# New engine rules in a planner, and its order of instructions searched again, in an attention and maxout kernel on one core

## The chip, the cores and the metric

The kernel runs on one core of one Trainium2 chip. The metric is device time in microseconds (us) of one execution. A run executes the kernel several times; medians are compared.

## The reference, cut to what matters

There are 4 batches, 8 heads, 768 positions and a head width of 64. Heads 0, 2 and 6 attend to all earlier positions, the other five only to the first 4 positions and to a window of 64. What the heads give is laid side by side (3072 rows of 512) and goes through a maxout block.

```python
scores = q @ k.T / 8                      # per batch and head, masked: causal, or causal and (sink or window)
a = exp(scores - max); a /= sum(a)        # softmax
x = (a @ v) -> rows (batch, position), columns (head, width): 3072 x 512
g = maximum(x @ w1, x @ w2)               # 3072 x 1024
out = g @ w_out                           # 3072 x 512
```

The kernel uses max(h1, h2) = h2 + relu(h1 - h2), so that out = relu(x (w1 - w2)) w_out + x (w2 w_out).

## The kernel before, in words

**Work.** All of it stands in `tile_paired_heads`. Heads go in pairs: index `n` runs over 16 pairs (4 of each batch; `HP` is 4). A pair's kind says whether its heads are full (F) or streaming (S). For each pair:

- `prepare_qk` loads q and k in float32, casts them to bfloat16 (`qkf` to `qb`) and turns them so that the head width lies on the partitions (`qk`). The casts of batch 0 (`cast_first_qk`, 128x192 each) may run on GpSimd, VectorE or ScalarE; those of later batches (`cast_qk`, 128x768) run on GpSimd alone. Up to `n` = 4 TensorE turns them through PSUM and a copy takes them out (`unturn`); later pairs use a VectorE transpose (`turn_squares`). For streaming heads `mix_k` copies parts of `qk` into `kx`: two copies, on VectorE or GpSimd.
- `prepare_v` loads v and casts it into `vb` (`cast_first_v` or `cast_v`); `mix_v` makes two copies from `vb` into `vx` on GpSimd.
- `attend` queues score matmuls (`ps`, line 624; the masks of batch 0 are added as bias matmuls, line 598), the exponential on ScalarE (`at`, line 641), mask products on VectorE in the later batches (line 663), the matmuls with v (`po`, line 685), and on VectorE a reciprocal and two multiplications (lines 700 and 702), which give `x`.

At the end of each batch `x` is transposed, by TensorE (`turn_x`, line 718) or, in batch 3, by a VectorE transpose (line 728) and 16 small DMAs for each half (`regroup_x`). Then the rows go through `up` (`ph`, line 759), a relu on ScalarE or VectorE (`g`, lines 770 and 772), `down` (`pout`, line 786), a copy out of PSUM and a store. The weights are prepared on the way, while batch 0 runs: `prepare_w` loads quarters of w2 and w1, subtracts them (`subtract`, line 893, two pieces for each quarter, on VectorE or GpSimd) and casts w2 (`cast_w2`); `prepare_wo` casts w_out (`cast_wo`); `product` multiplies w2 by w_out (line 866). The functions for copies share two lines: 421 (VectorE or GpSimd) and 419 (ScalarE).

**Order.** Nothing is scheduled by the compiler; every engine executes its instructions in the order in which they were issued. That order comes from a planner in the kernel file, `Order`. Each step is an `Op` with a cost in us for each engine that may run it, its dependencies and a rank (the pair's number, mostly). `Order.plan` walks through a modelled time: an engine that is free takes the ready operation of lowest rank, on the engine on which it would end first; TensorE picks from named lists ("TX", "S", "W", "TQ", "F", "P"), and up to 33 us of the modelled time it may run unneeded matmuls from list "D" (line 900) where nothing else fits. Loads are issued by SyncE in the order of the program. The modelled times only set the order; on the chip semaphores make each instruction wait for its data.

`Order.vary` shifts ranks before the plan is made. For each number in `SEEDS` it draws 1 to 20 operations that don't belong to TensorE, and mostly adds a normally distributed shift to their ranks:

```python
        for seed in seeds:
            rng = random.Random(seed)
            for o in rng.sample(movable, rng.choice((1, 2, 4, 8, 20))):
                o.shift = o.shift + rng.gauss(0, 2.0) if rng.random() < 0.8 else 0.0
```

**VectorE and GpSimd in the planner before.** An `Op` can be marked `port`. Every GpSimd operation, marked or not, starts no earlier than 0.13 us before the end of the last `port` operation on VectorE; a `port` operation on VectorE starts no earlier than 0.13 us before the end of the last GpSimd operation. Marked are `subtract`, `cast_first_qk`, `cast_first_v`, `mix_k` and the mask products. An engine is free again when the whole cost of an operation has passed.

Of the kernel before, what the change touches and what calls it, by code (L numbers as in the profile page):

```python
# [16 lines left out]
ACT = mybir.ActivationFunctionType  # L17
# [93 lines left out]
def heads_of(slots):  # L111
# [9 lines left out]
TERMS_FROM = {("s", 1, 2): 0, ("d", 3): 128, ("d", 5): 128, ("s", 0, 0): 640}  # L121
WARM, FIRST, FIRST_LOADS = 90, 6, 3


SEEDS = (
# [6 lines left out]
)  # L132


class Op:


    def __init__(self, engine, cost, emit, deps=(), rank=0, tail=0.12, bank=False, issue=0.55, by="SP", single=False, port=False):
        self.cost = cost if isinstance(cost, dict) else {engine: cost}
        self.engine, self.emit, self.rank, self.tail = engine, emit, rank, tail  # L140
        self.deps, self.bank = [d for d in deps if d is not None], bank
        self.issue, self.by, self.single, self.port = issue, by, single, port
        self.end, self.ready, self.users = None, 0.0, []
        self.behind, self.followers = None, []


class Order:

# [57 lines left out]
    def plan(self, names, together=(), spare=(), until=0.0, slack=0.0, begin=None):  # L206
# [71 lines left out]
        while True:  # L278
            while waiting and waiting[0][0] <= t:
                pending.append(heapq.heappop(waiting)[2])  # L280
            times = [waiting[0][0]] if waiting else []
            done = False
            for e in ("ACT", "DVE", "POOL", "SP"):
                able = [o for o in pending if e in o.cost or (o.engine == "DMA" and o.by == e)]
                if not able:
                    continue
                if free[e] > t:
                    times.append(free[e])
                    continue
                for o in sorted(able, key=lambda o: (o.rank + o.shift, o.ready, o.number)):  # L290
                    if o.engine == "DMA":
                        free[e] = t + o.issue
                        start = max(free[e], free["DMA"])
                        free["DMA"] = start + o.cost["DMA"]
                        end = free["DMA"] + 0.75
                    else:
                        shared = e == "POOL" or e == "DVE" and o.port
                        begin = max(t, held["DVE" if e == "POOL" else "POOL"] - 0.13) if shared else t
                        end = begin + o.cost[e]
                        if any(max(free[x], t) + c < end for x, c in o.cost.items() if x != e):  # L300
                            continue
                        free[e] = end
                        if shared:
                            held[e] = end
                    pending.remove(o)
                    steps.append((o, e, None))
                    release(o.followers, t)
                    finish(o, end)
                    done = True
                    break  # L310
            if free["PE"] <= t:
                best = pick()
                if best and best[1] <= t:
                    n = best[0]
                    now = t
                    for k in range(2 if n in together and not self.lists[n][at[n]].single else 1):
                        mine = self.lists[n][at[n]:at[n] + 1]
                        w = when(mine[0]) if mine else None
                        if w is None or w > now + 0.3:
                            break  # L320
                        o = mine[0]
                        at[n] += 1
                        bank = None
                        if o.bank:
                            bank = free_bank()[1]
                            users[bank] = o.bank
                        steps.append((o, "PE", bank))
                        now += o.cost["PE"] * (2 if now < self.warm else 1)
                        finish(o, now)
                    free["PE"] = now  # L330
                    done = True
                elif best:
                    times.append(best[1])
            else:
                times.append(free["PE"])
            if done:
                continue
            later = [x for x in times if x > t]
            if not later:
                break  # L340
            t = min(later)
# [6 lines left out]
def tile_paired_heads(tc, q, k, v, w1, w2, wo, out, qkf, vf, tab, idle, heads):  # L348
# [561 lines left out]
    def prepare_w(c, rank):  # L910
        loaded = load(1.5, load_w2(c))
        old, frees = take("qn")
        T["w1f", c] = slot("qn")[:, 0:KC * 256].rearrange("p (c f) -> p c f", c=KC)
        o = load(1.5, load_w1(c), old)
        for two in range(2):
            subs[c, two] = op(
                None, {"DVE": 0.69, "POOL": 1.27}, subtract(c, two), [o, loaded], rank=rank, port=True,
            )
            frees.append(subs[c, two])
        cast = op(None, {"DVE": 0.7, "POOL": 1.05}, cast_w2(c), [loaded], rank=rank)  # L920
        w2_casts.append(cast)
        ev = op(None, {"DVE": 0.69, "ACT": 1.05}, take_w2(c), rank=rank)
        ev.deps = [pe("P", 0.6, turn_w2(c), [cast], bank=ev)]
        w2t_ops.append(ev)
# [4 lines left out]
    def prepare_qk(n, part=0):  # L929
        nb, rank = len(parts_of[n][part]), rank_of(n, part)  # L930
        old, bfrees = take("qb")
        if n < HP:
            for ts in ((0,), (1,)):
                cost = {"POOL": 0.35, "DVE": 0.28, "ACT": 0.36} if len(ts) == 1 else {"POOL": 0.52, "DVE": 0.36, "ACT": 0.52}
                mine = [
                    op(
                        None, cost, cast_first_qk(n, part, hh, ts),
                        [*(first[part][t] for t in ts), *old], rank=rank, port=True,
                    ) for hh in range(2)
                ]  # L940
                for t in ts:
                    casts[n, part, t] = mine
                    first_frees[part][t].extend(mine)
        else:
            qn_old, frees = take("qn")
            T["qn", n, part] = slot("qn").rearrange("p (t s) -> p t s", t=2)
            cost, issue = (0.55, 0.52) if n < TURNED else (1.32, 1.14)
            mine = {
                (t, hh): load(cost, load_qk(n, part, t, hh), [*qn_old, sorted_], issue=issue)
                for t in range(2) for hh in range(2)  # L950
            }
            for t in range(2):
                casts[n, part, t] = [
                    op("POOL", 0.84, cast_qk(n, t), [mine[t, 0], mine[t, 1], *old], rank=rank)
                ]
                frees.extend(casts[n, part, t])
# [15 lines left out]
            ready.append(un)  # L972
        if "S" in KINDS[n] and part + 1 == len(parts_of[n]):
            cost = {"DVE": 0.5, "POOL": 0.92} if nb == NB else {"DVE": 0.4, "POOL": 0.6}
            ready.append(op(None, cost, mix_k(n), [*ready], rank=rank, port=True))
        k_ready[n] = [*k_ready.get(n, ()), *ready]

    def prepare_v(n, part=0):
# [3 lines left out]
        if n < HP:  # L982
            mine = [
                op(
                    None, {"POOL": 0.35, "DVE": 0.29}, cast_first_v(n, part, hh),
                    [first[part][2], *done_with["v", n][0]], rank=rank, port=True,
                ) for hh in range(2)
            ]
            first_frees[part][2].extend(mine)
        else:  # L990
            old, frees = take("vn")
            T["vn", n, part] = slot("vn").rearrange("p (h n d) -> p h n d", h=2, d=D)
            loads = [load(0.84, load_v(n, part, hh), [*old, sorted_], issue=0.57) for hh in range(2)]
            mine = [op("POOL", 0.84, cast_v(n), [*loads, *done_with["v", n][0]], rank=rank)]
            frees.extend(mine)
        v_ready[n] = [*v_ready.get(n, ()), *mine]
        if "S" in KINDS[n] and part + 1 == len(parts_of[n]):
            cost = (0.49 if KINDS[n] == "FS" else 0.78) * (1 if nb == NB else 0.7)
            v_ready[n] += [
                op("POOL", cost, mix_v(n, lower), [*mine], rank=rank) for lower in (True, False)  # L1000
            ]

    frees_ps = []
# [34 lines left out]
    def weigh(n, half, rank):  # L1038
# [17 lines left out]
        if p == HP - 1 and b >= SQUARES_FROM:  # L1056
# [6 lines left out]
            if half == 1 or not whole:  # L1063
# [2 lines left out]
                    op(  # L1066
                        "DMA", 0.5 if whole else 0.25, regroup_x(b, rows, g, a),
                        [*turned[b], *done_with["xt", b][0]], rank=n + 4 * half, issue=0.66,
                        by=("SP", "ACT")[a % 2], tail=0.5,
                    ) for g in range(4) for a in range(4)  # L1070
                ]
                done_with["xs", b][1].extend(moved)
# [11 lines left out]
    def prepare_wo(c, rank):  # L1084
        old, frees = take("qn")
        T["wof", c] = slot("qn")[:, 0:2 * d_model].rearrange("p (e f) -> p e f", e=2)
        o = load(1.4, load_wo(c), old)
        cost = {"ACT": 1.05, "DVE": 0.7, "POOL": 1.2}
        wob_ops.append(op(None, cost, cast_wo(c), [o], rank=rank))
        frees.append(wob_ops[-1])  # L1090

    def prepare_first(part, n):
# [668 lines left out]
```

## Time and profile before

| what | value |
|---|---|
| median of 3 runs | 184.31 us (183.98 to 184.77) |
| the profiled execution | 184.63 us |
| its span, first to last instruction | 182.8 us |
| granted TensorE clock | 0.998 |
| TensorE (PE) busy | 171.7 us, 94% of the span |
| VectorE (DVE) busy | 117.9 us, 65% |
| ScalarE (ACT) busy | 108.3 us, 59% |
| GpSimd (POOL) busy | 66.4 us, 36% |

How to read it: the profile is one execution. The span is 1.83 us shorter than the time of that execution, which in turn is 0.32 us above the median. Busy time counts an instruction from start to end, so pipelined matmuls that overlap count once. "PEld" is TensorE's loading of weights, "SPq" SyncE's queue of DMA issues. Of a wait the profile names the instruction that came last.

### The profile page before, as it was taken

How to read it: one execution, taken by the hardware profiler on the slowest of the kernel's cores; microseconds unless marked ns; L12 is line 12 of the kernel's file. 1: busy time of each engine (PE TensorE's matmuls, PEld its weight loads, DVE VectorE, ACT ScalarE, POOL GpSimd, SP SyncE). 2: the span in 40 equal slices, each digit the busy share in tenths (PEclk: the TensorE clock that was granted, in tenths of full speed). 3: DMA queues.
4: the chain of work that ended last, by engine and by line, in shares of the span. 5: the costliest groups of instructions: out<-in, count | busy, mean ns of one | idle time of the engine just before them, and what ended most of it. 6: DMA issues, size and time to landing. Idle time of an engine off the chain costs nothing.

```text
span 182.8 us, 4751 instructions
## 1 busy us (share of the span) xinstructions
PE 171.7 (94%) x1683; PEld 97.0 (53%) x1683; DVE 117.9 (65%) x265; ACT 108.3 (59%) x163; POOL 66.4 (36%) x108
## 2 busy tenths in 40 slices
PE   6899897989999899999989999999999999999990
PEld 1365564556454455566445655666555545545460
DVE  2687959991397789899798989979767632000000
ACT  3197797866956267875736695899673300526410
POOL 2244687504354955345774356683000000000000
PEclk9999999999999999999999999999999999999999
DMA  5999999699899799799998998999112368312032
GB/s 173 307 266 351 230 322 387 218 308 258 139 171 198 118 196 204 127 192 170 177 191 163 152 194 159 158 346 403 37 57 113 43 64 170 74 73 103 0 117 72
DMA packets 120674, 32.90 MB, mean 180 GB/s; under 512 B 107586, under 2 KB 116546, under 8 KB 120642
## 3 DMA queue, kind: packets, MB, share of 16 engines
q1 hardware_dynamic: 113954, 31.73, 74.6%
q10 hardware_dynamic: 6688, 0.79, 2.9%
q8 instruction: 15, 0.25, 0.6%
q14 instruction: 17, 0.14, 0.3%
HBM read 25.43 MB, written 6.29 MB: 174 GB/s over the span
## 4 chain that ended last, share of the span: by engine, by line
PE 58%; SPq 17%; DMA 12%; DVE 5%; issue 4%; POOL 2%; ACT 0%; POOLq 0%
PE pout L786 23%; PE ph L759 19%; SPq L476 9%; SPq L1616 7%; PE ps L624 5%; PE po L685 4%; DMA w2f<-in_moe_w_dram 3%; DMA vf<-in_v_dram 3%; DMA qkf<-in_q_dram 3%; PE po L866 3%; DMA qkf<-in_k_dram 2%; SPq L487 2%; PE pout L801 1%; DVE kx L421 1%; PE px L718 1%
## 5 line engine op out<-in xcount | busy, mean ns | idle before, releaser
L641 ACT ACTIVATE at<-ps 128x1024 bf16<-128x1024 f32 (+2 forms) x64 | 59.9, 978 | 12.5 <-PE ps L624 12.4
L759 PE MATMUL ph<-xt,w 128*128 128x384 bf16 x256 | 45.8, 326 | 1.1 <-DVE x L702 1.0
L786 PE MATMUL pout<-wob,g 128*128 128x512 bf16 x184 | 44.8, 379 | 0.0
L770 ACT ACTIVATE g<-ph 128x384 bf16<-128x384 f32 x56 | 26.8, 491 | 22.5 <-DMA out_dram<-ot 11.1
L421 POOL CAST qb<-qkf 128x768 bf16<-128x768 f32 (+1 forms) x37 | 24.1, 661 | 32.3 <-DMA qkf<-in_k_dram 17.1
L759 PEld LDWEIGHTS <-w 128*128 128x128 bf16 x256 | 23.6, 98 | 16.8 <-DVE x L702 1.3
L663 DVE TENSOR_TENSOR at<-at,tab 128x1024 bf16<-128x1024 bf16 (+5 forms) x45 | 27.3, 633 | 4.5 <-ACT at L641 4.2
L786 PEld LDWEIGHTS <-g 128*128 128x128 bf16 x184 | 16.7, 98 | 18.2
L702 DVE TENSOR_TENSOR x<-po,rez 128x192 f32 x64 | 22.9, 358 | 2.4 <-DVE x L702 0.2
L564 DVE STREAM_TRANSPOSE qk<-qb 128x768 bf16<-128x768 bf16 x22 | 20.8, 963 | 5.0 <-POOL qb L421 5.0
L786 PE MATMUL pout<-w2o,xt 128*128 128x512 bf16 x92 | 23.7, 380 | 0.0
L685 PEld LDWEIGHTS <-at 128*128 128x128 bf16 x477 | 19.1, 98 | 7.2 <-issue 0.5
L624 PE MATMUL ps<-qk 64*128 64x128 bf16 (+2 forms) x307 | 21.7, 234 | 0.0
L685 PE MATMUL po<-vb,at 128*128 128x65 bf16 x387 | 21.7, 194 | 0.1
L421 DVE COPY ot<-pout 128x512 f32<-128x512 f32 (+1 forms) x4 | 2.5, 625 | 29.3 <-PE pout L801 23.4
L421 POOL CAST vb<-vf 128x768 bf16<-128x768 f32 (+1 forms) x21 | 13.7, 666 | 17.5 <-DMA vf<-in_v_dram 13.2
L624 PEld LDWEIGHTS <-qk 64*128 64x128 bf16 x307 | 11.6, 94 | 13.2 <-issue 10.6
L421 POOL COPY vx<-vb 64x650 bf16<-64x650 bf16 (+3 forms) x24 | 16.3, 682 | 1.2
L419 ACT COPY ot<-pout 128x512 f32<-128x512 f32 (+1 forms) x9 | 5.1, 562 | 16.0 <-PE pout L786 12.0
L786 PEld LDWEIGHTS <-xt 128*128 128x128 bf16 x92 | 8.2, 98 | 8.5 <-issue 0.2
L624 PE MATMUL ps<-qk,kx 64*128 64x128 bf16 x91 | 9.2, 216 | 2.6 <-POOL kx L421 1.7
L772 DVE TENSOR_SCALAR g<-ph 128x384 bf16<-128x384 f32 x8 | 4.4, 555 | 7.0 <-PE ph L759 6.9
(66 smaller groups left out, 152.7 us busy)
## 6 DMA issues: line engine op xcount, KB each, us to landing
vf<-in_v_dram SPq DMA_DIRECT2D x24, 192.0 KB, 3.4
qkf<-in_q_dram SPq DMA_DIRECT2D x44, 96.0 KB, 3.2
qkf<-in_k_dram SPq DMA_DIRECT2D x44, 96.0 KB, 2.4
out_dram<-ot SPq DMA_DIRECT2D x11, 256.0 KB, 2.0
w2f<-in_moe_w_dram SPq DMA_DIRECT2D x4, 512.0 KB, 7.3
qkf<-in_moe_w_dram SPq DMA_DIRECT2D x4, 512.0 KB, 9.0
qkf<-in_moe_w_out_dram SPq DMA_DIRECT2D x4, 512.0 KB, 4.5
out_dram<-w2f SPq DMA_DIRECT2D x8, 256.0 KB, 4.5
```

Source lines behind the costliest of these rows:

```text
L421: eng[e].tensor_copy(out=out, in_=in_)
L476: dma[e].dma_start(out=dst[64 * hh + a:64 * hh + a + 32].rearrange("p (j e) -> p j e", e=32), in_=src[:, :, a:a + 32].rearrange("o (j p) e ...
L564: nc.vector.transpose(T["qk", n][:, t], T["qb", n, 0][:, t])
L624: nc.tensor.matmul(ps[:, bank, e * 128:(e + wide) * 128], lhsT=lhsT, rhs=qk[rows, 0, i * 128:(i + wide) * 128], start=bank not in begun, s ...
L641: nc.scalar.activation(out=at[:, 0:len(w), 0:w[0]], in_=T["ps", n, t][:, 0:len(w), 0:w[0]], func=ACT.Exp, scale=scale,)
L663: eng[e].tensor_tensor(out=at, in0=at, in1=tbl, op=ALU.mult)
L685: nc.tensor.matmul(po[:, hh, b[-1] - 3 * half, :], lhsT=at[:, bank, e * 128:(e + 1) * 128], rhs=rhs, start=first and (bank, hh, e, b) == m ...
L702: nc.vector.tensor_tensor(out=T["x", b][:, 3 * half:3 * half + 3, bass.ds(heads[PLACES[n][hh]], 1), :], in0=po[:, hh, :, 0:D].unsqueeze(2) ...
L759: nc.tensor.matmul(ph, lhsT=w12[:, kc, fc * 128:(fc + 1) * 128], rhs=xts[b % len(xts)][:, 3 * tg:3 * tg + 3, kc, :], start=(kc == 0), stop ...
L770: nc.scalar.activation(out=g[:, fc, :], in_=ph, func=ACT.Relu)
L786: nc.tensor.matmul(pout, lhsT=lhsT, rhs=rhs, start=(e == 0), stop=(e == len(steps) - 1))
L1616: lambda engine, dst=dst, src=src: engine.dma_start(out=dst, in_=src) for dst, src in pieces
```

## The change

The planner's rules and some costs are changed, and 67 numbers are put behind the 80 of `SEEDS`. No function that emits instructions is changed; the tiles, the sizes and the work are the same. What can differ on the chip is the order on each engine, and for operations with several engines, which one runs them.

- A new mark `shy`. A GpSimd operation waits for VectorE's `port` operations in the model only if it is `shy`: `subtract`, `mix_k`, `cast_first_v`, `cast_v` and `mix_v` are. The GpSimd casts `cast_qk`, `cast_first_qk`, `cast_w2` and `cast_wo` no longer wait. VectorE's `port` operations still wait for any GpSimd operation.
- `cast_w2` and `cast_wo` become `port`; `cast_first_qk` no longer is.
- An engine is free again a little before an operation's end: 0.1 us on ScalarE, 0.08 us on VectorE, 0.05 us on GpSimd.
- Costs: `cast_first_qk` on VectorE from 0.28 to 0.345 us, `cast_first_v` on VectorE from 0.29 to 0.28 us, `cast_wo` on GpSimd from 1.2 to 1.05 us; the time after a `regroup_x` DMA from 0.5 to 1.2 us.

```diff
+OVERLAP = {"ACT": 0.1, "DVE": 0.08, "POOL": 0.05}
...
-    230371,
+    230371, 7, 12, 23, 30, 37, 50, 56, 63, 71, 77, 81, 96, 103, 131, 133, 156, 211, 221, 229, 261,
...
+    442954, 442986, 443032, 443084, 443252,
...
-                        shared = e == "POOL" or e == "DVE" and o.port
-                        begin = max(t, held["DVE" if e == "POOL" else "POOL"] - 0.13) if shared else t
+                        other = {"POOL": "DVE" if o.shy else None, "DVE": "POOL" if o.port else None}.get(e)
+                        begin = max(t, held[other] - 0.13) if other else t
                         end = begin + o.cost[e]
                         if any(max(free[x], t) + c < end for x, c in o.cost.items() if x != e):
                             continue
-                        free[e] = end
-                        if shared:
+                        free[e] = end - OVERLAP[e]
+                        if e == "POOL" or e == "DVE" and o.port:
                             held[e] = end
...
-                None, {"DVE": 0.69, "POOL": 1.27}, subtract(c, two), [o, loaded], rank=rank, port=True,
+                None, {"DVE": 0.69, "POOL": 1.27}, subtract(c, two), [o, loaded], rank=rank, port=True, shy=True,
...
-        cast = op(None, {"DVE": 0.7, "POOL": 1.05}, cast_w2(c), [loaded], rank=rank)
+        cast = op(None, {"DVE": 0.7, "POOL": 1.05}, cast_w2(c), [loaded], rank=rank, port=True)
...
-                cost = {"POOL": 0.35, "DVE": 0.28, "ACT": 0.36} if len(ts) == 1 else {"POOL": 0.52, "DVE": 0.36, "ACT": 0.52}
+                cost = {"POOL": 0.35, "DVE": 0.345, "ACT": 0.36}
...
-                        [*(first[part][t] for t in ts), *old], rank=rank, port=True,
+                        [*(first[part][t] for t in ts), *old], rank=rank,
...
-            ready.append(op(None, cost, mix_k(n), [*ready], rank=rank, port=True))
+            ready.append(op(None, cost, mix_k(n), [*ready], rank=rank, port=True, shy=True))
...
-                    None, {"POOL": 0.35, "DVE": 0.29}, cast_first_v(n, part, hh),
-                    [first[part][2], *done_with["v", n][0]], rank=rank, port=True,
+                    None, {"POOL": 0.35, "DVE": 0.28}, cast_first_v(n, part, hh),
+                    [first[part][2], *done_with["v", n][0]], rank=rank, port=True, shy=True,
...
-            mine = [op("POOL", 0.84, cast_v(n), [*loads, *done_with["v", n][0]], rank=rank)]
+            mine = [op("POOL", 0.84, cast_v(n), [*loads, *done_with["v", n][0]], rank=rank, shy=True)]
...
-                op("POOL", cost, mix_v(n, lower), [*mine], rank=rank) for lower in (True, False)
+                op("POOL", cost, mix_v(n, lower), [*mine], rank=rank, shy=True) for lower in (True, False)
...
-                        by=("SP", "ACT")[a % 2], tail=0.5,
+                        by=("SP", "ACT")[a % 2], tail=1.2,
...
-        cost = {"ACT": 1.05, "DVE": 0.7, "POOL": 1.2}
-        wob_ops.append(op(None, cost, cast_wo(c), [o], rank=rank))
+        cost = {"ACT": 1.05, "DVE": 0.7, "POOL": 1.05}
+        wob_ops.append(op(None, cost, cast_wo(c), [o], rank=rank, port=True))
```

More of the change, by code (lines that the diff above doesn't have):

```diff
@@ L130, with __init__ @@
     101142, 101161, 101196, 101554, 101575, 101777, 101808, 101856, 102175, 102430, 102706, 230301,
[1 row of a table removed]
[5 rows of a table added]
 )
 class Op:
-    def __init__(self, engine, cost, emit, deps=(), rank=0, tail=0.12, bank=False, issue=0.55, by="SP", single=False, port=False):
+    def __init__(self, engine, cost, emit, deps=(), rank=0, tail=0.12, bank=False, issue=0.55, by="SP", single=False, port=False, shy=False):
         self.cost = cost if isinstance(cost, dict) else {engine: cost}
@@ L141, in __init__ @@
         self.deps, self.bank = [d for d in deps if d is not None], bank
-        self.issue, self.by, self.single, self.port = issue, by, single, port
+        self.issue, self.by, self.single, self.port, self.shy = issue, by, single, port, shy
         self.end, self.ready, self.users = None, 0.0, []
```

3 rows, old and new, of the table SEEDS are left out of this document.

## The prediction

> **What bounds the kernel now.** I read the page first. TensorE is the bound: busy 94% of the span, with its full clock in every slice, and the chain that ended last closes with its matmuls.
>
> ```profile
> PE 171.7 (94%) x1683; PEld 97.0 (53%) x1683; DVE 117.9 (65%) x265; ACT 108.3 (59%) x163; POOL 66.4 (36%) x108
> PEclk9999999999999999999999999999999999999999
> ```
>
> The order changes neither number nor size of the needed matmuls, so only TensorE's waits can go or come. I then asked for the busy time by stretches, from its first needed matmuls (about 9 us) to its last (178.4 us); the columns after the length are PE, PEld, DVE, ACT and POOL busy.
>
> ```profile
> 9.00:20.00 11.00, 10.51 (x150) 6.42 (x150) 8.98 (x28) 8.96 (x17) 4.45 (x14) 1.00 1.15 307
> 20.00:30.00 10.00, 8.89 (x137) 5.58 (x138) 7.91 (x20) 8.64 (x11) 8.94 (x20) 1.00 1.01 299
> 30.00:40.00 10.00, 8.92 (x110) 5.92 (x109) 9.79 (x19) 7.22 (x13) 3.22 (x3) 1.00 0.82 285
> ...
> 60.00:70.00 10.00, 9.33 (x88) 4.90 (x87) 8.13 (x17) 4.95 (x6) 7.51 (x11) 1.00 0.94 160
> ...
> 90.00:100.00 10.00, 8.94 (x93) 4.74 (x92) 9.20 (x19) 5.01 (x5) 6.78 (x9) 1.00 0.99 180
> ```
>
> TensorE's idle time is 0.49 + 1.11 + 1.08 + 0.67 + 1.06 = 4.41 us; the stretches left out have none. That is all an order can win, save three unneeded matmuls between 11 and 14 us, about 0.2 us each. The timeline of TensorE shows the four large waits:
>
> ```profile
> 28.89 0.23 PE L624 MATMUL ps<-qk,kx 64*128 64x128 bf16 x2 [0.89 <-DVE kx L421]
> 37.18 0.82 PE L759 MATMUL ph<-xt,w 128*128 128x384 bf16 x4 [0.95 <-DVE x L702]
> 64.06 0.23 PE L624 MATMUL ps<-qk,kx 64*128 64x128 bf16 x1 [0.67 <-POOL kx L421]
> 92.07 0.23 PE L624 MATMUL ps<-qk,kx 64*128 64x128 bf16 x1 [1.06 <-POOL kx L421]
> ```
>
> Last I read what VectorE and GpSimd did ahead of them.
>
> ```profile
> 26.93 1.18 DVE L421 CAST w2b<-w2f 128x1024 bf16<-128x1024 f32 x1 [1.28 <-DMA w2f<-in_moe_w_dram]
> 32.86 3.37 DVE L893 TENSOR_TENSOR w<-qkf,w2f 128x512 bf16<-128x512 f32 x3
> 89.36 2.34 DVE L663 TENSOR_TENSOR at<-at,tab 128x768 bf16<-128x768 bf16 x2
> 89.61 0.82 POOL L421 CAST qb<-qkf 128x768 bf16<-128x768 f32 x1
> 90.50 1.52 POOL L421 COPY kx<-qk 64x320 bf16<-64x320 bf16 x2
> ```
>
> Two kinds of delay can be seen: a queue whose head waits for a load (the 1.28 us before w2b), and VectorE and GpSimd standing in each other's way. The w2b cast took 1.18 us; the cast of w_out of the same size took 0.69 us on VectorE. The three subtractions took 3.37 us; alone one takes 0.67. The kx copies took 1.52 us; the same two took 0.85 us at 63 us. The cast at 89.61 kept its 0.82 us while the masks beside it were late: the first took 1.48 us, where the shortest of its size takes 0.52.
>
> **The change part by part.** The sum goes against the profiled execution: 184.63 us, of which 182.8 are the span. It was 0.32 us above the median of 184.31, and the median gets the difference.
>
> *Does the new rule fit the rows better?* Of the 24 GpSimd casts of 128x768 to qb, 23 took 0.82 to 0.83 us whatever VectorE did; one took 1.00, at 70.8 us beside a mask. VectorE's casts of 128x192 to qb took 0.342 to 0.354 us with GpSimd's equal casts running beside them (at 6.0, 8.5 and 17.0 us): the old plan forbade that and priced them at 0.28; the new one allows it at 0.345. Masks and copies on VectorE do wait for GpSimd: over their shortest durations, kx copies (0.23) took 1.33 and 1.31 us more twice, a mask of 128x512 (0.38) 1.33 more. The early release fits too: two VectorE casts start 0.26 us apart at 0.34 each, and a pair of 0.35 us on GpSimd starts 0.29 apart. So the planner's clock for these two engines now stands nearer the chip's.
>
> The Trainium skill, in "SBUF — State Buffer", section "Who interferes with whom", says that VectorE and GpSimd share one port pair, that the first to take it holds it for the whole instruction, and that the other fully blocks. By that a GpSimd cast would wait for a mask that began first, against the new rule; the row at 70.8 us agrees, where 0.17 us was added.
>
> *Terms.*
> 1. The wait at 28 us: the planner of before let w2b run on VectorE without regard to GpSimd; it now waits, so its real price is seen. Worth 1.18 - 0.69 = 0.49 of the 0.89; the rest is the late load, which no edit prices anew.
> 2. The wait at 92 us: the casts in front of kx no longer queue behind masks in the plan, and the masks do behind casts. Worth 1.52 - 0.85 = 0.67 of the 1.06.
> 3. The wait at 37 us: the subtractions were marked for contention already. One stood for 1.76 us beside a GpSimd subtraction of 1.27 that had itself waited 0.40 us for its load. Bounds 0 and 0.95; I take 0, since that rule is as before.
> 4. The wait at 64 us: kx ran at its undisturbed 0.85 us, behind a cast whose data had just landed. I take 0 of 0.67.
> 5. 9 to 20 us: waits of 0.49 and fillers of 0.6. Landings of q, k and v set most of the pace (VectorE and GpSimd both start at 12.15 to 12.18 us, when v lands). Bounds 0 and 1.1; I take 0.3, nearer to no gain.
> 6. New waits: every later order is redrawn by 67 new seeds and by the free times, and loads land as before. Bounds: none, or two of the largest seen, 2.1 us. I take one of the small kind, 0.2, as the early waits on casts were (0.20, 0.22, 0.23).
> 7. The regroup's 1.2 us tail, and the costs of w_out's and first v's casts: 0. The 16 first regroup DMAs (0.59 to 0.75 us of issue each but for two, on two queues, after a transpose that begins at 140.07) land by about 149.8 us; TensorE is busy until 152.3 with rows of batch 2, so 2.5 us of cover. If that cover is gone, each us beyond it costs one.
>
> Sum: -0.49 - 0.67 - 0.30 + 0.20 = -1.26. The profiled execution would come to 183.37 us, the median to 184.31 - 1.26, about 183.05. Item 7 is also a ceiling: unless attention ends earlier, TensorE gains at most 2.5 us before it waits for the regroup, which gives 181.8.
>
> **The rivals.**
> - *The waits only move* (a seed removes one kx wait and puts another operation before the next). For it: the waits at 28 and 64 us begin with a load, whose costs are unchanged, and a shift that helps one copy delays another. Against it: after 40 us TensorE waits in two places only, 1.7 us in 138, so there is other work to put in front. Terms 1, 2 and 5 give 1.46 and new waits of 1.3 take it back: 184.15.
> - *The casts do wait.* The port rule holds whenever a mask begins first, and the plan, believing otherwise, packs casts beside masks. The largest such loss in the rows is a cast of v at 59.4 us, 1.22 instead of 0.83 us: 0.39. Two such ahead of the two kx chains cost 0.8: -1.26 + 0.8, so 183.9. Against it: only 5 of 36 large casts lost anything, 0.05 to 0.39 us each.
> - *Slower: a weight piece stands at the head of VectorE's queue before it has landed.* From 19 to 41 us VectorE or GpSimd must do 8 subtractions, 4 casts of w2 and some of w_out, and behind them wait kx, the reciprocals and x. The new plan frees VectorE 0.08 us earlier for each of some 60 operations by then, yet its loads are priced as before, so it reaches these pieces with the loads where they were. It happened once: 1.28 us of waiting became 0.89 on TensorE, whose remaining work there is short. From about 0.4 us (1.28 - 0.89) of lateness on it reaches TensorE. Two more such waits at 0.89 to 0.95 each, with nothing won: 184.31 + 1.84, 186.15. For it: DMA share is 1.0 there and w2 took 7.3 us to land. Against it: the pieces may also go to GpSimd, idle 6.8 of the 10 us from 30 to 40.
>
> **How the numbers follow.** About 0.5% (0.9 us) is what a measurement of this kernel can tell from no change. Forecast, faster: 0.53; its own range is 181.8 (ceiling) to 183.4. Waits only move: 0.11; casts do wait: 0.07; both lie within 0.5%, together 0.18. Slower by weight pieces: 0.29. It has a good chance since nothing in the new rules prices landings, and two of the four large waits start there. The range runs from the ceiling to near the slower rival: 181.7 to 186.0.
>
> **What would show it.** If right: no wait over 0.5 us on kx near 28 and 92 us; the two-copy kx groups nearer to 0.85 us; fewer VectorE rows stretched beyond 1.3 us; more GpSimd casts beside VectorE casts before 20 us; TensorE idle 9 to 178 us near 3.2 us. If slower: a new bracketed DMA wait of VectorE between 19 and 41 us, and a TensorE wait behind it. It would be wrong in kind if TensorE waited at the first rows of batch 3 for the regroup, or if its unneeded matmuls (18 now) grew past 20 us.

## The result, and the profile after

The kernel after takes 185.66 us (median of 22 runs, 184.28 to 187.78), the kernel before 184.53 us in the runs beside it. The ratio is 1.0065 with a 95% interval of 1.0036 to 1.0094: slower, by less than 1% but clear of no change. The ratios and their intervals are taken from executions within 1.5% of the fastest of the same kernel, the medians from all. The profiled execution took 184.81 us, its span is 183.0 us.

Of the after kernel's page, the same two lines as before, which show almost no change (23 of TensorE's matmul records are missing in this trace, 1660 instead of 1683, so its busy time is a little low, here and in the stretches that follow):

```profile
PE 171.0 (93%) x1660; PEld 97.4 (53%) x1682; DVE 115.2 (63%) x273; ACT 108.2 (59%) x165; POOL 63.1 (34%) x98
PEclk9999999999999999999999999999999999999997
```

Of the after kernel's windows, the same stretches (columns: PE, PEld, DVE, ACT, POOL busy, then granted clock, DMA share, GB/s):

```profile
9.00:20.00 11.00, 9.66 (x144) 6.05 (x145) 8.34 (x29) 9.08 (x18) 3.29 (x11) 1.00 1.15 307
20.00:30.00 10.00, 8.26 (x111) 5.18 (x111) 9.23 (x22) 8.09 (x12) 6.11 (x12) 1.00 0.98 283
30.00:40.00 10.00, 9.62 (x143) 6.93 (x141) 9.65 (x22) 7.29 (x11) 6.27 (x6) 1.00 0.86 311
...
60.00:70.00 10.00, 9.89 (x89) 4.90 (x89) 6.28 (x18) 5.52 (x8) 6.02 (x10) 1.00 0.90 154
70.00:90.00 20.00, 18.99 (x239) 11.62 (x237) 18.06 (x38) 14.71 (x21) 9.46 (x12) 1.00 0.96 169
90.00:100.00 10.00, 8.99 (x85) 4.73 (x84) 9.76 (x24) 5.30 (x7) 5.48 (x9) 1.00 0.96 172
```

TensorE gains 0.70 us from 30 to 40 us and 0.56 from 60 to 70. It loses 0.85 from 9 to 20, 0.63 from 20 to 30 and 1.01 from 70 to 90 us, where it had been busy throughout; the waits that its timeline names there are 0.75 us of the 1.01, the rest may be missing records. The timeline shows the large waits of after. The four shown of before are gone or below 0.25 us, but near 92 us another stands in place of the one for kx:

```profile
16.37 0.34 PE L557 MATMUL pt<-tab,qb 128*128 128x128 bf16 x3 [0.72 <-POOL qb L428]
23.74 0.33 PE L557 MATMUL pt<-tab,qb 128*128 128x128 bf16 x3 [1.59 <-DVE qk L428]
88.92 0.81 PE L766 MATMUL ph<-xt,w 128*128 128x384 bf16 x4 [0.43 <-DVE g L779]
92.00 0.20 PE L692 MATMUL po<-vb,at 128*128 128x65 bf16 x1 [0.79 <-DVE at L670]
```

VectorE's rows ahead of that last wait:

```profile
89.78 0.56 DVE L428 COPY kx<-qk 64x320 bf16<-64x320 bf16 x2
90.37 1.57 DVE L670 TENSOR_TENSOR at<-at,tab 128x1024 bf16<-128x1024 bf16 x1
```

The longest, before 23.74, is a turn that needs a PSUM bank, which VectorE's copy to `qk` frees. What VectorE, and then GpSimd, did ahead of it (timeline of the kernel after):

```profile
21.43 1.79 DVE L900 TENSOR_TENSOR w<-qkf,w2f 128x512 bf16<-128x512 f32 x1 [0.64 <-DMA qkf<-in_moe_w_dram]
23.14 0.54 DVE L428 COPY qk<-pt 128x384 bf16<-128x384 bf16 x1
23.61 0.67 DVE L428 COPY xt<-px 128x1024 bf16<-128x1024 bf16 x1
```

```profile
21.41 1.27 POOL L900 TENSOR_TENSOR w<-qkf,w2f 128x512 bf16<-128x512 f32 x1 [0.30 <-DMA qkf<-in_moe_w_dram]
```

VectorE has its first subtraction at the head of its queue before the w1 piece has landed and waits 0.64 us for it. The same landing releases GpSimd's subtraction of the other half; GpSimd starts 0.02 us earlier, runs its usual 1.27 us, and VectorE's takes 1.79 instead of about 0.7. The copies that TensorE waits for stand behind it. In the kernel before, VectorE did them first:

```profile
21.00 1.02 DVE L421 COPY qk<-pt 128x384 bf16<-128x384 bf16 x2
22.02 1.08 DVE L421 COPY xt<-px 128x1024 bf16<-128x1024 bf16 x2
23.01 0.73 DVE L893 TENSOR_TENSOR w<-qkf,w2f 128x512 bf16<-128x512 f32 x1
```

That profile shows no drop of the clock near 25 us, and its time is 0.18 us above the profiled execution of before. It is one of 3 among 22 runs whose mean granted clock was 0.992 or more; the other 19 lay below. The experiments show what that is.

### The profile page after: what moved, and what is told of

The parts are those of the page before. It is cut to its first block, busy times and chain, and to the rows that moved or that the text cites. A ratio compares the mean times of both kernels' runs of the same rounds, so it can differ in the third digit from the quotient of the medians.

```text
span 183.0 us, 4723 instructions
## 1 busy us (share of the span) xinstructions
PE 171.0 (93%) x1660; PEld 97.4 (53%) x1682; DVE 115.2 (63%) x273; ACT 108.2 (59%) x165; POOL 63.1 (34%) x98
## 4 chain that ended last, share of the span: by engine, by line
PE 51%; SPq 17%; DMA 15%; DVE 7%; issue 5%; POOL 2%; ACT 0%; POOLq 0%; DVEq 0%
PE pout L793 23%; PE ph L766 16%; SPq L483 11%; DMA vf<-in_v_dram 6%; DMA qkf<-in_moe_w_dram 5%; PE po L692 4%; PE ps L631 4%; SPq L494 3%; SPq L1623 3%; DVE at L670 2%; DMA qkf<-in_k_dram 2%; DMA qkf<-in_q_dram 2%; DVE w L900 2%; PE pout L808 1%; POOL qb L428 1%
## 5 line engine op out<-in xcount | busy, mean ns | idle before, releaser
L793 PE MATMUL pout<-wob,g 128*128 128x512 bf16 x176 | 43.2, 379 | 0.5
L777 ACT ACTIVATE g<-ph 128x384 bf16<-128x384 f32 x50 | 24.5, 492 | 7.6 <-PE ph L766 7.4
L670 DVE TENSOR_TENSOR at<-at,tab 128x1024 bf16<-128x1024 bf16 (+5 forms) x45 | 26.2, 601 | 2.8 <-ACT at L648 2.7
L426 ACT COPY ot<-pout 128x512 f32<-128x512 f32 (+1 forms) x11 | 6.2, 567 | 30.5 <-PE pout L793 15.9
L793 PE MATMUL pout<-w2o,xt 128*128 128x512 bf16 x84 | 22.7, 379 | 0.5 <-issue 0.2
L692 PEld LDWEIGHTS <-at 128*128 128x128 bf16 x477 | 18.3, 97 | 8.0 <-DVE at L670 2.2
L428 DVE COPY ot<-pout 128x512 f32<-128x512 f32 (+1 forms) x2 | 1.1, 558 | 31.2 <-PE pout L808 29.1
L428 POOL CAST vb<-vf 128x768 bf16<-128x768 f32 (+1 forms) x16 | 11.6, 730 | 17.8 <-DMA vf<-in_v_dram 9.2
L779 DVE TENSOR_SCALAR g<-ph 128x384 bf16<-128x384 f32 x14 | 7.7, 551 | 6.0 <-PE ph L766 5.1
L426 ACT COPY w2f<-pout 128x512 f32<-128x512 f32 x7 | 4.1, 586 | 9.5 <-PE pout L793 9.5
```

The costliest lines, as they stand in the source:

```text
L426: nc.scalar.copy(out=out, in_=in_)
L428: eng[e].tensor_copy(out=out, in_=in_)
L670: eng[e].tensor_tensor(out=at, in0=at, in1=tbl, op=ALU.mult)
L692: nc.tensor.matmul(po[:, hh, b[-1] - 3 * half, :], lhsT=at[:, bank, e * 128:(e + 1) * 128], rhs=rhs, start=first and (bank, hh, e, b) == m ...
L777: nc.scalar.activation(out=g[:, fc, :], in_=ph, func=ACT.Relu)
L793: nc.tensor.matmul(pout, lhsT=lhsT, rhs=rhs, start=(e == 0), stop=(e == len(steps) - 1))
```

## The experiments

Theory A at the start: the loss is the wait near 22 us, made by the subtraction's place. Rivals: the seeds' new order elsewhere, and GpSimd's casts. The traces leave little to the casts: 31 of the 36 GpSimd casts of 128x768 take 0.82 to 0.83 us in `after` as in before, and all 36 together 31.0 us instead of 30.6. Each ratio is against the kernel before, run on the same chip.

**Rules or seeds.** `rules_only` is the kernel after with the 80 numbers of before in `SEEDS`; `seeds_only` is the kernel before with all 147.

> The changed kernel with the 80 seeds of before: the new rules and costs alone. If the rules themselves make the order worse: ratio 1.004 or more. If the new rank shifts do: ratio within 0.004 of 1. The order is a third one, so the place of its waits decides; theory A expects a wait of over 0.8 us only where VectorE or GpSimd reaches a weight piece or a first cast ahead of its landing.

> The kernel before with all 147 seeds under the old rules. The added shifts were not chosen for these rules, so they act as random ones: I expect waits like those of any order, 5 to 7 us of TensorE's idle time after 9 us, ratio 1.002 to 1.012. If the added seeds alone carry the loss, its ratio is at least that of the change, 1.0065.

Measured: 187.06 us, 1.0144 (1.0091 to 1.0196), and 186.46 us, 1.0146 (1.0102 to 1.0191). `rules_only` has the same meeting at 21.43 and 21.45 us, and TensorE waits 1.94 us behind it:

```profile
21.45 1.79 DVE L896 TENSOR_TENSOR w<-qkf,w2f 128x512 bf16<-128x512 f32 x1 [0.85 <-DMA qkf<-in_moe_w_dram]
```

So the rules and costs put the subtraction there, not the seeds. `seeds_only` has no such place and no TensorE wait over 0.96 us; its last matmul ends at 180.3 us against 178.4 before. Its trace shows where most of that can lie: it runs 24 unneeded matmuls instead of 18, some of them among needed ones at 23 to 24 us:

```profile
23.13 0.78 PE L904 MATMUL unused<-idle,tab 128*128 128x512 bf16 x2
24.17 0.39 PE L904 MATMUL unused<-idle,tab 128*128 128x512 bf16 x1
```

From 9 us on they take 3.00 us of TensorE, against 1.15 before. Such time counts as busy and is no wait. A run of this order without them was not made, so this stays argued. Each half alone measures worse than both together.

**The subtraction's place.** `later` moves it in after behind the copies, in the list of steps that `Order.run` emits; `early` moves it in before ahead of two qk copies and the x copy.

```diff
+        steps.insert(141, steps.pop(124))      # later
+        steps.insert(123, steps.pop(144))      # early
```

> The changed kernel with one VectorE subtraction (first weight quarter, first piece) moved in VectorE's order from ahead of the qk and x copies at 21.4 us to behind them and the kx copy; nothing else moves. Theory A (VectorE waits 0.64 us for the landing of w1 and then 1.1 us behind GpSimd's subtraction, and TensorE's 1.59 us wait at 22 us comes from it): that wait falls under 0.4 us and the time comes back by 1.2 to 1.6 us, to a ratio of 0.998 to 1.002 against the kernel before. Theory B (the loss lies in many small waits or in a lower granted clock): under 0.4 us, ratio 1.004 to 1.008.

> The kernel before with the same subtraction moved the other way, ahead of the two qk copies and the x copy, to the place that it has in the changed order. Theory A: a TensorE wait of 0.8 to 1.6 us appears between 21 and 24 us, ratio 1.004 to 1.009. Theory B: no wait over 0.4 us there, ratio within 0.002 of 1.

Measured: `later` 184.37 us, 0.9998 (0.9963 to 1.0034), so this one move takes the whole loss back. VectorE's subtraction, now behind the copies, waits for nothing and is short:

```profile
22.88 0.72 DVE L901 TENSOR_TENSOR w<-qkf,w2f 128x512 bf16<-128x512 f32 x1
```

The wait at 22 us is gone, but the gain is not there either: two other waits come up. One is 1.38 us before 33.41, where GpSimd's copies to vx stand behind a cast of w2 that waited 4.40 us for its load. The other is 0.94 us before 38.73, behind a later subtraction of VectorE that takes 1.74 us because GpSimd's, at 35.66, began 0.07 us ahead of it. `early` 184.51 us, 0.9997 (0.9961 to 1.0034): no loss. There VectorE started first, at 21.20, and GpSimd's subtraction was the one that took 1.77 us:

```profile
21.20 0.69 DVE L894 TENSOR_TENSOR w<-qkf,w2f 128x512 bf16<-128x512 f32 x1 [0.19 <-DMA qkf<-in_moe_w_dram]
...
21.25 1.77 POOL L894 TENSOR_TENSOR w<-qkf,w2f 128x512 bf16<-128x512 f32 x1 [0.54 <-DMA qkf<-in_moe_w_dram]
```

The early place alone is thus no loss here, though VectorE waited only 0.19 us for the landing, less than in after. Whether it becomes one when GpSimd goes first is the next question.

**Who goes first.** `win` leaves after's order but gives GpSimd an unneeded 0.52 us memset ahead of its subtraction, so that VectorE starts first. `both` adds a second memset ahead of the GpSimd cast of `qk` data at 90.6 us, so that VectorE's mask there starts before it; `both_again` is `both` once more; `again` is the kernel after.

```diff
+        late = steps[133][0]                    # win; both: also steps[524][0]
         for o, e, self.bank in steps:
+            if o is late:
+                self.hold()                     # nc.gpsimd.memset(spare, 0.0), 128x512 bf16
             o.emit(e)
```

> The changed kernel with one unneeded memset (128x512, about 0.5 us) on GpSimd ahead of its first subtraction, so that VectorE's subtraction, released by the same landing, starts first. If the loss at 22 us is mostly the shared port: VectorE's subtraction takes 0.7 instead of 1.8 us, TensorE's wait there falls from 1.59 to 0.4 to 0.7, ratio 0.999 to 1.004. If it is mostly the late landing: the wait stays over 1.2 us and the ratio at 1.004 to 1.009.

> As the run with one spare memset, with a second one on GpSimd ahead of the cast that follows the vx copies at 90.6 us, so that VectorE's mask gets the port between them. Theory A for that place: the mask of 1.57 us takes under 1.1, TensorE's wait of 0.79 us at 91 us falls under 0.3, ratio 0.003 to 0.005 under the run with one memset. Rival: the wait there comes from late loads of k, and stays.

> The changed kernel itself once more, for a second profile and a ratio on the same chip as the three beside it. All theories: ratio 1.004 to 1.009. Theory A (weight pieces at the heads of queues, with VectorE and GpSimd falling on one landing): a TensorE wait between 21 and 24 us of either about 0.4 us, where VectorE's subtraction takes 0.7, or about 1.6, where it takes 1.8.

> The changed kernel with the two spare memsets, once more. It had 0.9975 with an interval on both sides of 1. Theory A: ratio 0.993 to 0.999, both subtractions' order and the mask at 90 us as in its first profile. Rival: it is no better than the kernel before, 0.999 to 1.003.

Measured on one chip: `again` 185.44 us, 1.008 (1.0041 to 1.0118); `win` 184.67, 0.9991 (0.9946 to 1.0037); `both` 184.42, 0.9975 (0.9926 to 1.0024). `both_again`, later: 185.17, 1.0029 (0.9987 to 1.0071). In `win` VectorE's subtraction takes 0.69 us and GpSimd's 1.73:

```profile
21.41 0.69 DVE L903 TENSOR_TENSOR w<-qkf,w2f 128x512 bf16<-128x512 f32 x1 [1.30 <-DMA qkf<-in_moe_w_dram]
22.02 0.55 DVE L431 COPY qk<-pt 128x384 bf16<-128x384 bf16 x1
```

The landing's share of the wait stays (VectorE waited 1.30 us for it; TensorE 1.15, between the two values that were expected, and 2.39 in `again`), and the meeting goes VectorE's way. With it most or all of the loss goes: the medians of `win` and `both`, which share the first memset, are 0.77 and 1.02 us below `again`. The kernel before had a median of 183.94 us beside them, so a rest of up to half a per cent is not excluded. The second memset did what it should to the mask (0.79 instead of 1.57 us), but the two measurements of `both` lie on both sides of 1: its worth is not resolved, and `both_again` fell short of the 0.993 to 0.999 that was expected.

**The same meeting in the kernel before.** `blocked` moves VectorE's subtraction in before to step 131 instead of 123; `lose` is `early` with an unneeded VectorE memset ahead of the subtraction. Both were meant to let GpSimd's subtraction go first.

> The kernel before with its first VectorE subtraction moved ahead of one qk copy and the x copies, but behind another qk copy, so that GpSimd's subtraction has started when VectorE arrives. In the run where it was moved two copies further ahead VectorE started first (0.69 us) and the time did not change. If the shared port is the price: VectorE's subtraction takes 1.3 to 1.8 us, a TensorE wait of 0.8 to 1.5 us appears at 22 to 24 us, ratio 1.003 to 1.008. If only the landing matters: no wait over 0.5 us there, ratio within 0.003 of 1.

> The kernel before with its first VectorE subtraction moved early, as in the run where that cost nothing (VectorE started 0.05 us ahead of GpSimd), and one spare memset (128x512 float32) on VectorE ahead of it, so that GpSimd starts first. If losing the port is what costs the time: GpSimd's subtraction takes 1.27 us, VectorE's 1.5 to 1.8, a TensorE wait of 1.0 to 1.8 us stands at 21 to 24 us, ratio 1.004 to 1.009. If the place in the queue alone matters: like the run before without the memset, ratio within 0.003 of 1.

Measured: 184.08 us, 1.0006 (0.9969 to 1.0043), and 184.57 us, 1.0007 (0.9967 to 1.0048). Neither met its premise: in before's order GpSimd has two kx copies ahead of its subtraction, VectorE went first in both, and no wait over 0.4 us followed by 24 us. They say only that before's order tolerates an early subtraction. That the meeting lost by VectorE costs time is thus shown in after's order alone.

**The clock.** The repetition of the kernel after shows what its own profile lacks. Windows of `again` (after the POOL column, the granted clock):

```profile
22.00:24.00 2.00, 0.23 (x3) 0.15 (x2) 2.00 (x3) 0.89 (x1) 1.45 (x2) 1.00 0.89 193
24.00:26.00 2.00, 2.00 (x22) 1.41 (x20) 1.94 (x6) 1.10 (x2) 1.16 (x4) 0.75 1.05 341
26.00:28.00 2.00, 2.00 (x12) 0.93 (x12) 1.48 (x5) 1.07 (x2) 1.35 (x5) 0.50 1.07 379
28.00:30.00 2.00, 2.00 (x17) 0.86 (x15) 1.66 (x5) 0.99 (x3) 1.23 (x2) 0.90 1.09 378
```

After a TensorE wait of 2.39 us, longer than either value expected of `again`, the clock is granted at half for (1 - 0.75) x 4 + 2.0 + (1 - 0.90) x 4 = 3.4 us. Four `ph` matmuls take 1.46 us there:

```profile
23.77 0.33 PE L557 MATMUL pt<-tab,qb 128*128 128x128 bf16 x3 [2.39 <-DVE qk L428]
...
26.84 1.46 PE L766 MATMUL ph<-xt,w 128*128 128x384 bf16 x4
```

In the kernel after's own profile the same four take 0.82 us. Half speed for 3.4 us of 183 is a mean clock of 0.991, so runs below 0.992 can be counted as runs with such a stretch. The count is rough: the clock also falls after the last matmul, where it costs TensorE nothing, and this alone gives the 0.994 of the kernel after's own profile; the kernel before has at most 2 of 17 to 35 runs below 0.992. Three kernels on one chip then asked whether the idle time itself does it. `fill` is after with eight unneeded repeats of the last three transposes before the wait; `hole` is before with three unneeded VectorE memsets ahead of its qk copies; `again_2` is after.

```diff
+            if o is late:                       # fill: behind step 131 of after
+                self.hold()                     # 8 x 3 transposes of qb into the same pt
...
+            if o is late:                       # hole: ahead of step 123 of before
+                self.hold()                     # 3 x nc.vector.memset(spare, 0.0), 128x512 f32
```

> The kernel after, with eight unneeded repeats of the three turns that TensorE does last before its wait at 22 us (24 transposes of 128x128 into the same PSUM tile, about 0.17 us for each three). VectorE's and GpSimd's order stays: subtraction behind GpSimd's, qk and x copies late. Theory A (the loss is mostly the half-speed clock that follows a TensorE idle of 1.6 to 2.4 us): TensorE is busy in the wait with unneeded work, the idle stretch shrinks to below 1 us, the granted clock is above 0.992 in nearly all runs, and the ratio to the kernel before falls to 0.998 to 1.003, though no needed matmul starts earlier. Theory B (the loss is the wait itself, that is that the copies come late): the ratio stays at 1.004 to 1.009.

> The kernel before, with three spare VectorE memsets (128x512 float32, about 0.65 us each) ahead of its qk copies at 21 us: the same hole in TensorE's work, made by other means, with nothing of the change and with GpSimd and the loads untouched. Theory A (a TensorE idle of 1.6 us or more here brings the half-speed clock): TensorE waits 1.5 to 2.2 us for qk near 22 us, most runs show a granted clock below 0.992 and the profile a stretch of about 3.4 us at 0.5 near 24 to 28 us; ratio 1.010 to 1.020, more than the wait alone. Theory B (the clock has another cause, for instance the order of the loads or the engines' collision): the clock stays at 0.998 and the ratio is at most that of the wait, 1.004 to 1.011.

> The kernel after once more, on the chip of the two kernels beside it, so that their clocks and times can be set against it. Both theories: ratio 1.004 to 1.012, a granted clock below 0.992 in most runs, TensorE's wait near 22 us 1.5 to 2.4 us.

Measured: `again_2` 185.70 us, 1.0054 (1.0014 to 1.0093), 7 of 12 runs below 0.992. `fill` 185.16 us, 1.002 (0.9986 to 1.0054), none of 12; TensorE's idle fell to 0.89 us although its needed work started as late as ever:

```profile
21.44 1.50 PE L1198 MATMUL pt<-tab,qb 128*128 128x128 bf16 x24
23.83 0.33 PE L560 MATMUL pt<-tab,qb 128*128 128x128 bf16 x3 [0.89 <-DVE qk L431]
```

`hole` made TensorE wait only 0.35 and 0.81 us, below its premise: 184.83 us, 1.0006 (0.997 to 1.0042), one of 12 runs below 0.992. `hole_5` has five memsets.

> The kernel before, with five spare VectorE memsets instead of three ahead of its qk copies at 21 us. With three TensorE stood idle for 0.35 and 0.81 us only; two more at 0.66 us each make the second wait about 2.1 us, as long as the one of the kernel after. Theory A (an idle of this length brings the half-speed clock, whatever made it): granted clock below 0.992 in half of the runs or more; ratio 1.008 to 1.016. Theory B (the clock falls for another reason that belongs to the changed order): at most two of twelve runs below 0.992, as in the kernel before; ratio 1.003 to 1.010.

Measured: 186.33 us, 1.0074 (1.0044 to 1.0105), and 10 of 12 runs below 0.992; the kernel before beside it had 1 of 23. The clock is as theory A has it; the ratio lies just under its range and inside that of theory B. TensorE's timeline and the windows of `hole_5`:

```profile
25.17 0.38 PE L721 MATMUL px<-tab,x 128*128 128x128 bf16 x4 [2.64 <-DVE qk L424]
```

```profile
26.00:28.00 2.00, 1.64 (x20) 1.06 (x17) 1.69 (x6) 1.19 (x2) 0.44 (x1) 0.65 1.09 386
28.00:30.00 2.00, 2.00 (x11) 1.03 (x10) 0.47 (x1) 1.02 (x1) 1.91 (x6) 0.50 1.09 381
```

The idle brings the half clock, whatever made it: here nothing of the change is present, and in `fill` all of it is, without the long idle and without the slow clock. The slow stretch is again (1 - 0.65) x 4 + 2.0 = 3.4 us.

**Loads priced as they land.** In `landed` the planner with after's rules gets other costs for the loads of w1 and w2 and for one of v, chosen by their landings in the traces, and 22 other numbers behind the 80 old seeds; `landed_b` has 15 other ones, `landed_again` is `landed` once more.

```diff
-        loaded = load(1.5, load_w2(c))
+        loaded = load((1.5, 3.2, 1.5, 1.7)[c], load_w2(c))
-        o = load(1.5, load_w1(c), old)
+        o = load((2.6, 1.8, 1.3, 1.5)[c], load_w1(c), old)
-                FIRST_TAKES[t] / len(mine), lambda e, move=move: move(dma[e]), issue=1.0 if t < 2 else 0.6
+                (2.55 if (part, t) == (1, 2) else FIRST_TAKES[t]) / len(mine), lambda e, move=move: move(dma[e]), issue=1.0 if t < 2 else 0.6
```

> The changed rules with the loads of the first 40 us priced at about where the profiles show them landing (the first w1 quarter 1.1 us later than in the changed planner, later weight quarters 1.9 to 2.6 us), and the rank shifts searched again from the 80 old seeds with 22 new ones. Theory A (the rules are sound, the landings were the hole): VectorE no longer stands at the first subtraction before its landing, TensorE has no wait over 0.8 us between 19 and 36 us, ratio 0.985 to 0.997. Rival (a plan's gain doesn't reach the chip at this size): ratio 0.998 to 1.008.

> As the one before, with 15 other new seeds from another search, a second draw. Its order still has VectorE and GpSimd at the two first subtractions at once, behind a qk copy. Theory A: ratio 0.985 to 0.999; the rival: 0.998 to 1.008.

> The planner with the rules after, loads priced as they landed, and the 80 old and 22 of other seeds, once more. It was 0.9971 with an interval of 0.9935 to 1.0008 against the kernel before. If that was a gain: again below 0.9985. If it was noise: 0.998 to 1.003.

Measured: `landed` 184.29 us, 0.9971 (0.9935 to 1.0008); `landed_b` 185.79, 1.0028 (0.9993 to 1.0062); `landed_again` 184.07, 0.9939 (0.9903 to 0.9975). None of these 36 runs lies below 0.992. VectorE's first subtraction in `landed`, and TensorE's busy time:

```profile
20.38 0.56 DVE L418 COPY qk<-pt 128x384 bf16<-128x384 bf16 x1
20.86 1.01 DVE L418 COPY xt<-px 128x1024 bf16<-128x1024 bf16 x2
21.79 1.01 DVE L418 COPY qk<-pt 128x384 bf16<-128x384 bf16 x2
22.72 0.68 DVE L890 TENSOR_TENSOR w<-qkf,w2f 128x512 bf16<-128x512 f32 x1
```

```profile
20.00:30.00 10.00, 9.70 (x158) 6.48 (x158) 9.80 (x31) 8.39 (x12) 5.59 (x11) 1.00 0.99 290
30.00:40.00 10.00, 9.93 (x105) 6.83 (x102) 8.36 (x17) 8.63 (x15) 3.11 (x3) 1.00 0.91 317
```

The copies go first, the subtraction waits for nothing, and TensorE idles 0.37 us from 20 to 40 us against 2.19 before. The second measurement puts `landed` ahead of the kernel before, the first agrees in sign; the gain is 0.3 to 0.6%. `landed_b`, with the same costs, lies between before and after and is told apart from neither, so the costs alone don't make a gain; that still hangs on the seeds. In its trace VectorE's first subtraction again waits for nothing, but it runs 1.96 us of unneeded matmuls from 9 us on, where `landed` has 0.77.

## Why the prediction was wrong, point by point

The forecast was 183.05 us and faster; the kernel came out at 185.66 and slower. That lies inside the stated range only because its upper end was drawn from the slower rival. What happened is the slower rival's mechanism, a weight piece at the head of VectorE's queue before it has landed, with a bracketed DMA wait of VectorE and a TensorE wait behind it near the low end of the 19 to 41 us that were named. Step by step:

- *Term 1 (w2b, 28 us), right in kind.* w2b takes 0.67 us on VectorE at 28.52 and waits for nothing. TensorE's wait of 0.89 is gone, more than the 0.49 taken.
- *Term 2 (kx, 92 us), not reliably won.* The kx copies went to VectorE and take 0.56 us, but the mask behind them, beside GpSimd's copies to vx and its cast, takes 1.57 us, and TensorE waits 0.79 us for it, after 0.43 for a relu. That is 1.22 for the 1.06 that went, where the sum had a gain of 0.67. In `again_2` it is 0.25 and 1.02; in `again` neither wait is there.
- *Term 3 (the wait at 37 us, "since that rule is as before"), wrong in its reason.* The wait itself is gone, where the sum took nothing. But the subtractions' rule did not change, and their places did (`rules_only`): VectorE reached the first one before the landing, and GpSimd stood ready for the other half. The term priced a subtraction only where it stood in the old order. Which of the new rules or costs moved it was not tried apart.
- *Term 4 (64 us), better than taken:* the wait of 0.67 us is gone.
- *Term 5 (9 to 20 us), not won:* TensorE is busy 9.66 us instead of 10.51 in the profiled execution, with some records missing. GpSimd's casts of q wait for their load there and start at 15.38 us, where those of the kernel before start at 14.75, which gives the wait before 16.37. `again` and `again_2` have no such wait and are busy 10.64 and 10.43 us, so about nothing was won or lost.
- *Term 6 (new waits, 0.20), the step that failed.* One wait alone was 1.59, 2.39 and 1.92 us in three profiles of this kernel, eight to twelve times the 0.20 taken. It lay within the bounds of 0 to 2.1 or just above them; the small value was the wrong end. It was also misread: of the three early waits that it stands on, only the one of 0.23 us is for a cast. The term says itself that loads land as before while the order is redrawn, and still left out what the slower rival made of it. And waits were priced at their length: the clock behind them was not in the sum.
- *Term 7, right:* the regroup cost nothing; there is no wait of TensorE at batch 3's first rows. The other sign of being wrong in kind did not come either: there are 17 unneeded matmuls, the last at 12.5 us.

The size, as far as the runs part it. Of 46 runs of the kernel after (`after`, `again`, `again_2`), 35 lie below a clock of 0.992 and average 185.89 us; the 11 others average 185.04. So the slow stretch is worth about 0.85 x 35 / 46 = 0.65 us of the mean, an estimate and a rough one: taken singly, the three measurements put the 0.85 at 1.50, 0.43 and 0.62. `fill`, with a median 0.54 us below `again_2`, says about the same, though their intervals overlap. The medians of after and before are 1.13 us apart, so perhaps half of the loss is the clock. The other half is there without it. The late copies are the likely cause, since `later` takes back both, but `fill`, which has the late copies and no slow clock, is not told apart from the kernel before.

The slower rival asked for two waits at 0.89 to 0.95 and "nothing won". There was one long wait, then the clock, and the gains of terms 1 and 4 stood against them; that its 186.15 came near is in part luck. Its argument against itself, that the pieces "may also go to GpSimd", turned out to make it worse: GpSimd took half of the piece, and went first. Its point of decision, a lateness of about 0.4 us, agrees: VectorE waited 0.64, 1.43 and 0.96 us for the landing.

"The waits only move" holds for the rest. With the meeting at 22 us removed (`later`) the time is that of before: the waits that went at 28, 37, 64 and 92 us were replaced by others.

The port rule that the prediction weighed, in the Trainium skill's "SBUF — State Buffer", section "Who interferes with whom", was applied to casts beside masks. It decided at the subtractions: where VectorE began first (`early`, `win`) it kept its 0.69 us and GpSimd took 1.77 and 1.73; where GpSimd began first (`after`) it kept its 1.27 and VectorE took 1.79. The traces agree with it but for a little: after GpSimd's end VectorE's took only 0.54 us more, less than its 0.69.

## What to carry to other kernels

New engine rules in a planner can bring a load-fed operation to the head of a queue before its data has landed, so when they change, its load times need the same look; what stands behind that operation is what pays. Two engines that both stand ready for halves of one piece start at the same landing and block each other: put the path's copies ahead of both, or let the faster one start first. Price a wait of TensorE near 2 us and above with the clock after it, not by its length alone, and look at the granted clock of all runs, since the one profiled may be without it. Where unneeded work may fill gaps, count it beside the waits: it shows as busy time.

## What the runs showed of the hardware

- *Half clock after a short idle.* TensorE waits of 1.94, 2.39 and 2.64 us (`rules_only`, `again`, `hole_5`) were each followed by one stretch of 3.4 us at a granted clock of 0.50, which began between the wait's end and about 1.4 us after it. In the 3.4 us just ahead of the stretch TensorE was idle for 1.90, 2.19 and 2.05 us, more than half of them. Waits of 1.59 and 1.92 us in the profiles of `after` and `again_2` had none, but 35 of 46 runs of that kernel show it in their mean clock; waits of 0.81, 1.15 and 1.38 us (`hole`, `win`, `later`) go with 1, 2 and 0 of 12. Whether half of such a stretch is the limit was not tried. The Trainium skill, "TensorE: Matmul & The Clock Gate", section "What's actually happening", gives half speed after at least one idle window of about 3.4 us, with a window that runs free of the kernel. The length of the stretch and its coming in some runs only agree with that; the idle that sufficed here was 0.8 to 1.5 us shorter.
- *Who wins an equal release.* In `after`, `again`, `again_2`, `rules_only` and `fill` GpSimd's subtraction starts 0.02 to 0.03 us before VectorE's on the same landing. In `early` VectorE was 0.05 us ahead. Why is open.
